# Six positions instead of five in the last column transform: the second MLP layer of two hidden units moved there

## The chip, the cores and the metric

One core of one Trainium2 chip runs the kernel. The metric is the time of one execution on the device in microseconds, here the median of three runs. TensorE (PE) multiplies matrices, VectorE (DVE) and ScalarE (ACT) do elementwise work and move results out of the accumulators, GpSimd (POOL) and SyncE (SP) mostly issue DMA transfers.

## The reference

A layer norm feeds two branches, which are added to the input: the real part of a two-dimensional Fourier transform, and an MLP with a gelu. S = 2048 rows, D = 640 columns, F = 1536 hidden units.

```python
x = A_x                                     # (1, 2048, 640)
xn = _layernorm(x, axis=-1)
a = xn @ dft_hid_re ; b = xn @ dft_hid_im
y = dft_seq_re @ a - dft_seq_im @ b
h = gelu(xn @ B_w1 + B_b1)
return x + y + (h @ B_w2 + B_b2)
```

## The kernel before

**Precision.** Each fp32 operand is split into a high part (a copy on ACT, `high`) and a low part (a subtraction on DVE, `low`, which reads the high part). A product (`product`, lines 298 to 303) is three matmuls into one accumulator: high x high, high x low of the moving operand, low x high of the weights. So the second matmul of a product needs the low part of the moving operand.

**Tiles.** The rows are cut into 4 row blocks of 512 (t = 0 to 3), the hidden units into 12 units of 128 (NF = 12), the columns into 5 chunks of 128 (ND = 5). A matmul has a 128x128 weight tile and a 128x512 moving tile. The second layer of one unit of one row block (`output`) is 5 chunks of one product each, 15 matmuls.

**Stages, in order.** (1) Row block 0 goes through the MLP plainly, unit by unit. (2) Row blocks 1 and 2 go through the first layer together: `pair(k)`, k = 0 to 5, makes units 2k and 2k+1 of both with sums and differences of operands, so that fewer matmuls do; seven `window` calls write three accumulator banks in turn. Of row block 1 the second layer is done inside the following pair (`put_out`); the hidden values of row block 2 are kept in DRAM (`gs`, by `keep`) and loaded again later (`load_unit`). Beside the pairs ACT and DVE prepare the forms of the column transform's matrix (`prep_w`, tiles named `wst`), which `beside_pair` calls at fixed places. (3) A loop over p = 0 to 13 does the rest of the second layer: p = 0 and 1 units 10 and 11 of row block 1, p = 2 to 13 units 0 to 11 of row block 2. Each iteration calls `output(g)` and then `split_unit(g + 2, units[p])`, which splits the unit that is wanted two iterations later. (4) Row block 3 goes through the MLP, while the forms of the sequence transform are built (`fourier_step`). (5) Sequence transform stages ("s") and column transform stages ("y") alternate, for pairs of row blocks; what the MLP left is added into the accumulators as seeds. The last "y" stage is that of row blocks 1 and 2.

**Beside the loop of (3).** `between(p)` makes the input of row block 3: statistics of the rows (`ln_stats` 12 to 15), the root on ACT (`ln_scale`, L224) and the normalization on DVE (`ln_apply`, L233) at p = 3, then 16 DMA transfers from SBUF to SBUF (`put_z`, L795, eight issued by SP and eight by POOL, tile `z`), 32x32 transposes on DVE (`transpose_z`, L261, `ztx`) and splits into `xt` (`prep_xt`) at p = 7, 8 and 9. It also stores seeds (partial sums, `keep_seed`), and reloads pieces of w1 (`load_w1`, `prep_w1`).

**The last column transform.** Seven products of sums are formed from the two row blocks' real and imaginary sequence sums (`form` makes and splits the moving operand of each). Each product has 5 positions along the contraction of 640 (two halves of 256 with two positions each, and an odd one of 128); its width in column chunks is (3, 3, 3, 2, 2, 2, 3), 18 in all (`GWIDE`). `hidden_entry` issues them; product 6's second chunk is done in two halves of 256 columns, so that the first half can leave early. `t2`, `t3`, `t4` form the sums on DVE.

What sets the order is the program text alone: each engine works through its instructions in the order in which the functions above issue them, and waits on semaphores. `place(name)` gives a region of SBUF a new use.

Of the kernel before, what the change touches and what calls it, by code (L numbers as in the profile page):

```python
# [22 lines left out]
PADL = 7  # L23


@with_exitstack
def kernel(
# [84 lines left out]
    seeds = dram.tile([P, 2 * ND, TB], F32, name="seeds")  # L112

# [193 lines left out]
    NG = NT * NF  # L307
    HT, oacc, xo = {}, {}, {}
# [56 lines left out]
    def output(g, es=range(ND)):  # L365
        t, i = divmod(g, NF)
        oacc[t] = [bank(k) for k in OBANKS[t]]
        hs = HT[g]
        for e in es:
            cols = slice(e * P, (e + 1) * P)  # L370
            product(
                oacc[t][e], (W2[i][:, 0, cols], W2[i][:, 1, cols]), (hs[:, 0], hs[:, 1]), i == 0, i == NF - 1
            )
# [589 lines left out]
    def keep(g, a):  # L963
        nc.gpsimd.dma_start(gs[g % NF], a)
# [42 lines left out]
    def beside_pair(k, at):  # L1007
# [54 lines left out]
        if k == LASTK and at == 7:  # L1062
            A["gs"] = place("xab3", (P, 5, TB), F32)
            for i in range(3, 6):
                load_unit(i)
        if k == LASTK and at == 2:
            for i in range(3):
                load_unit(i)
        if k == LASTK and at == 4:
            load_x(14)  # L1070
            load_x(15)
            for i in range(6, 8):
                load_unit(i)
            A["s1"] = place("xab2", (P, ND, TB), F32)
# [3 lines left out]
    def load_unit(i):  # L1078

        if i < NF:  # L1080
            units[i] = A["gs"][:, i - 3] if 3 <= i < 8 else early.tile([P, TB], F32, tag="w2r", bufs=3, name=f"g{i}")
            nc.sync.dma_start(units[i], gs[i])

    def pair(k):
# [13 lines left out]
        split_unit(a1, u, lambda _: high(zc, z_))  # L1098
# [25 lines left out]
        gelu(a2, x_)  # L1124
# [4 lines left out]
        for es in ((0, 1, 2), (3, 4)) if k == 0 else (range(ND),):  # L1129
            outputs.extend((g, e) for g in (a1, a2) for e in es)  # L1130

    def between(p):

        if p == 0:
            ln_stats(12)
            ln_stats(13)
        if p == 1:
            with_bias(A["s1"][:, 1], 1, 3)
            with_bias(A["s1"][:, 4], 1, 4)
            keep_seed("us", A["s1"][:, 4:])  # L1140
            ln_stats(14)
        if p == 2:
            ln_stats(15)
        if p == 3:
            ln_scale(NC)
            Z["z"] = zo_tile("z3")
            for c in range(3 * NC, 4 * NC):
                ln_apply(c)
            put_z(Z["z"], row_places, nc.gpsimd, nc.sync)
            new_xt(3)  # L1150
        if p == 4:
            with_bias(A["s1"][:, 0], 1, 2)
            keep_seed("x", A["s1"][:, :2])
        if p == 5:
            for e in range(2):
                less(A["s1"][:, 2 + e], 1, e, A["s1"][:, e])
            keep_seed("y", A["s1"][:, 2:4])
        for j in {7: (0,), 8: (1, 2), 9: (3, 4)}.get(p, ()):
            if j == 0:
                transpose_z("x30", Z["z"], 0)  # L1160
            if j + 1 < ND:
                transpose_z(f"x3{j + 1}", Z["z"], j + 1)
            prep_xt(f"x3{j}", j)
        if p == 11:
            open_place(*PLACES[3])
        if p == 12:
            open_place(*PLACES[2])
        for n in {0: (0,), 4: (1,), 5: (2,), 6: (3,), 7: (4,), 8: (5,), 9: (6,), 10: (7,), 11: (8,), 12: (9, 10), 13: (11,)}.get(p, ()):
            prep_w1(AGAIN[n], 2 * NF + n)
            load_w1(2 * NF + 3 + n)  # L1170
        if p in (0, 1, 4, 8):
            load_unit({0: 8, 1: 9, 4: 10, 8: 11}[p])
        if p == 10:
            put_rows(3, row_places, nc.sync)
        if p == 12:
# [61 lines left out]
    for p in range(2 + NF):  # L1237
        g = 2 * NF - 2 + p
        if p == NF:
            output(g)  # L1240
            gelu(g + 2, hidden(g + 2))
        elif p == NF + 1:
            acc = hidden(g + 2)
# [8 lines left out]
            gelu(g + 2, acc, fill)  # L1252
# [8 lines left out]
        else:  # L1261
            output(g, (3, 4, 0, 1, 2) if p == 1 else range(ND))
# [9 lines left out]
    for i in range(NF):  # L1272
        g = 3 * NF + i
        if i >= NF - 2:
            output(g)
        else:
            acc = hidden(g + 2)
            gelu(g + 2, acc)
            output(g)

        fourier_step(i)
# [109 lines left out]
    def seed(dst, src):  # L1391
        nc.scalar.activation(dst, src, AF.Copy)

    def beside(h, t, n):
# [108 lines left out]
        else:  # L1503
# [35 lines left out]
            if p == 3:  # L1539

                def load_d():
# [7 lines left out]
                    11: [lambda: seed(z_, A["seed"]), lambda: load_seeds("us", "vs")],  # L1549
# [42 lines left out]
    def hidden_beside(b, n):  # L1592
# [10 lines left out]

        def t2(k):
            return lambda: add(s(1, KU[k]), s(1, KV[k]), s(1, KU[k]), ALU.subtract)

        def t3(k):
            return lambda: add(s(0, KU[k]), s(1, KU[k]), s(0, KU[k]), ALU.subtract)

        def t4(k):  # L1610
            return lambda: add(s(0, KV[k]), s(0, KV[k]), s(1, KU[k]), ALU.subtract)
# [51 lines left out]
        def last_columns():  # L1663

            A["end"] = A["rt2"][:, 0, 0, 0]
# [56 lines left out]
        }.get(n, [])  # L1722
        sooner = 2 if last else 0
# [38 lines left out]
    def hidden_entry(n, b, w, u):  # L1762
        last = b == len(blocks) - 1
        where = (X, Y, Z, X, Z, X, X)[w]

        def use_g(acc, j, pos, first, stop, goes_on=False, rows=slice(None)):
            k = pos % 2
            a = form_slot(n - u + pos // 2)
            use(acc, GT[b, w * ND + pos], j, a, k, first, stop, goes_on, rows)

        def wide(j, pos):
            use_g(bank(where + j), j, pos, w < 3 and pos == 0 and not last, pos == ND - 1, w > 2 or last)

        mine = (2 * u, 2 * u + 1) if u < 2 else (4,)
        if w == 6 and last:

            if u == 0:
                for pos in range(ND):
                    use_g(bank(VS), 2, pos, False, pos == ND - 1, True)
                for pos in range(ND):  # L1780
                    wide(0, pos)
            elif u == 1:
                for acc, rows in zip((Y, X + 1), PARTS):
                    for pos in range(ND):
                        use_g(bank(acc)[:, rows], 1, pos, False, pos == ND - 1, True, rows)
# [7 lines left out]
        for pos in mine:  # L1793
            if w < 2:
                use_g(bank(US), 2, pos, w == 0 and pos == 0 and not last, w == 1 and pos == ND - 1, last)
# [4 lines left out]
        for pos in mine:  # L1800
# [80 lines left out]
```

## Time and profile before

| | |
|---|---|
| median of 3 runs | 850.13 us (849.91 to 850.81) |
| the profiled execution | 850.44 us |
| its span | 848.6 us |
| PE | 841.7 us busy, 3725 matmuls |
| DVE | 676.9 us, 889 instructions |
| ACT | 368.2 us, 527 instructions |
| POOL | 78.2 us, 142 instructions |

The span runs from the first to the last instruction of the profiled execution; its own time is 1.84 us longer. Row times are microseconds from the start of the span. In the timeline a row gives the start, the duration, the engine, the line, the operation and the tiles, with `x3` where like instructions follow each other. In the rows by group the two numbers behind the bar are the busy time in us and the mean of one instruction in ns. In the rows by stretch each engine has its busy time and its count, in the order PE, weight loads, DVE, ACT, POOL, then the granted clock of PE, the share of the DMA engines and GB/s. Matmul durations overlap: how fast PE goes is read from the starts.

### The profile page before, as it was taken

What the parts mean: (1) busy time and instruction counts of PE and PEld (TensorE: products, weight loads), DVE (VectorE), ACT (ScalarE), POOL (GpSimd) and SP (SyncE); (2) the same over time, 40 slices, a digit from 0 to 9 for tenths busy, and PEclk for the clock granted to TensorE, in tenths of its full rate; (3) what the DMA queues carried; (4) which work ended last, traced back from release to release, by engine and by line L of the source; (5) the groups of instructions that cost most, each with busy time, mean ns of one, the idle gap of its engine ahead of it and who ended that gap; (6) DMA issues with size and microseconds to landing.
All of it is one profiled execution on the core that took longest, in us unless ns stands there. A gap on an engine that the chain in (4) does not pass through costs nothing.

```text
span 848.6 us, 10664 instructions
## 1 busy us (share of the span) xinstructions
PE 841.7 (99%) x3725; PEld 696.9 (82%) x3725; DVE 676.9 (80%) x889; ACT 368.2 (43%) x527; POOL 78.2 (9%) x142
## 2 busy tenths in 40 slices
PE   9999999999999999999999999999999999999997
PEld 7888888888888888888888888888888888888886
DVE  6969989766643778979988887889967998886596
ACT  7546657545453555443444344232323433234340
POOL 3340024222200000000000000000000000000012
PEclk9999999999999999999999999999999999999999
DMA  7995767878785897958644679663845799916473
GB/s 232 280 251 153 151 178 246 261 223 305 198 220 139 344 313 143 204 129 190 152 137 110 165 226 285 158 147 96 224 142 156 229 246 245 310 43 229 149 192 88
DMA packets 193878, 167.33 MB, mean 197 GB/s; under 512 B 57792, under 2 KB 164800, under 8 KB 193312
## 3 DMA queue, kind: packets, MB, share of 16 engines
q1 hardware_dynamic: 182816, 136.89, 60.8%
q0 software_dynamic: 8832, 29.24, 10.1%
q10 hardware_dynamic: 2176, 0.52, 0.3%
q8 instruction: 29, 0.48, 0.2%
q14 instruction: 25, 0.20, 0.1%
HBM read 116.53 MB, written 46.14 MB: 192 GB/s over the span
## 4 chain that ended last, share of the span: by engine, by line
PE 99%; POOL 0%; DVE 0%; issue 0%; POOLq 0%
PE banks L302 30%; PE banks L303 30%; PE banks L304 29%; PE banks L322 10%; PE banks L685 1%; PE banks L701 0%; POOL warm L673 0%; POOL zeros L671 0%; DVE yo L1842 0%; PE banks L755 0%; POOLq masks.py:199 0%; POOLq L1867 0%
## 5 line engine op out<-in xcount | busy, mean ns | idle before, releaser
L188 ACT ACTIVATE as<-r 128x1024 fp32r<-128x1024 f32 x80 | 85.0, 1062 | 170.2 <-PE banks L304 146.4
L303 PE MATMUL banks<-as,xab 128*128 128x512 f32 (+1 forms) x389 | 150.5, 387 | 0.0
L304 PE MATMUL banks<-as,xab 128*128 128x512 f32 (+1 forms) x389 | 150.5, 387 | 0.0
L302 PE MATMUL banks<-as,xab 128*128 128x512 f32 (+1 forms) x389 | 150.5, 387 | 0.0
L191 DVE TENSOR_TENSOR as<-r,as 128x1024 fp32r<-128x1024 f32 x80 | 97.2, 1216 | 38.0 <-ACT as L188 37.8
L302 PE MATMUL banks<-as,xc 128*128 128x512 f32 x224 | 87.1, 389 | 0.0
L303 PE MATMUL banks<-as,xc 128*128 128x512 f32 x224 | 87.1, 389 | 0.0
L304 PE MATMUL banks<-as,xc 128*128 128x512 f32 x224 | 87.1, 389 | 0.0
L303 PEld LDWEIGHTS banks<-as,xab 128*128 128x128 f32 x389 | 73.0, 188 | 15.0
L302 PEld LDWEIGHTS banks<-as,xab 128*128 128x128 f32 x389 | 73.0, 188 | 14.8
L304 PEld LDWEIGHTS banks<-as,xab 128*128 128x128 f32 x389 | 73.0, 188 | 14.8
L188 ACT ACTIVATE as<-rt 128x1024 fp32r<-128x1024 f32 x32 | 34.0, 1062 | 72.5 <-PE banks L304 57.9
L322 PE MATMUL banks<-xt,xab 128*128 128x512 f32 x240 | 56.6, 389 | 0.0
L191 DVE TENSOR_TENSOR hs<-ab,hs 128x512 fp32r<-128x512 f32 x36 | 24.8, 689 | 38.0 <-ACT hs L188 37.5
L322 PEld LDWEIGHTS banks<-xt,xab 128*128 128x128 f32 x240 | 45.0, 188 | 9.3
L303 PEld LDWEIGHTS banks<-as,xc 128*128 128x128 f32 x224 | 42.0, 188 | 8.8
L304 PEld LDWEIGHTS banks<-as,xc 128*128 128x128 f32 x224 | 42.0, 188 | 8.7
L302 PEld LDWEIGHTS banks<-as,xc 128*128 128x128 f32 x224 | 42.0, 188 | 8.7
L302 PE MATMUL banks<-hs,xc 128*128 128x512 f32 x120 | 46.7, 389 | 0.0
L303 PE MATMUL banks<-hs,xc 128*128 128x512 f32 x120 | 46.7, 389 | 0.0
L304 PE MATMUL banks<-hs,xc 128*128 128x512 f32 x120 | 46.7, 389 | 0.0
L191 DVE TENSOR_TENSOR as<-rt,as 128x1024 fp32r<-128x1024 f32 x32 | 38.8, 1213 | 6.5 <-ACT as L188 6.5
(286 smaller groups left out, 1682.0 us busy)
## 6 DMA issues: line engine op xcount, KB each, us to landing
raw<-in_A_dft_seq_re_dram SPq DMA_DIRECT2D x64, 256.0 KB, 5.6
raw<-in_A_dft_seq_im_dram SPq DMA_DIRECT2D x64, 256.0 KB, 5.2
w1r<-in_B_w_dram SPq DMA_DIRECT2D x144, 80.0 KB, 3.1
wit<-wst POOLq DMA_DIRECT2D x15, 384.0 KB, 4.0
wit<-wst POOLq DMA_DIRECT2D x20, 256.0 KB, 4.2
forms_ab<-xab SPq DMA_DIRECT2D x4, 1280.0 KB, 7.7
xab<-wit SPq DMA_DIRECT2D x13, 384.0 KB, 4.8
row<-xn SPq DMA_DIRECT2D x14, 320.0 KB, 5.2
```

The source lines that it names most:

```text
L188: nc.scalar.activation(h, s, AF.Copy)
L191: nc.vector.tensor_tensor(l, s, h.bitcast(F32), op=ALU.subtract)
L302: nc.tensor.matmul(acc, wh, mh, start=first, stop=False, skip_group_check=goes_on)
L303: nc.tensor.matmul(acc, wh, ml, start=False, stop=False, skip_group_check=goes_on)
L304: nc.tensor.matmul(acc, wl, mh, start=False, stop=last, skip_group_check=goes_on)
L322: nc.tensor.matmul(acc, W1[i][:, a, j * P : (j + 1) * P], XT[j][:, b], start=n == 0, stop=n == len(steps) - 1)
L685: nc.tensor.matmul(wacc, warm[:, :P], warm, start=True, stop=True)
```

## The change

Units 10 and 11 (the last two, `NU = NF - 2 * NX` = 10 remain) of row blocks 1 and 2 no longer go through `output`. Their hidden values are written to DRAM (`late_units`) and loaded by POOL, with the two 128-row blocks of w2 that belong to them, at step 11 of the last sequence stage (`load_late`). In the last column transform they are a sixth position: they take the part that a real and an imaginary chunk take elsewhere, so `form` splits one more 128x512 tile for each of the seven products, `also` does the sums of `t2` to `t4` on the hidden values too, and `late_form` makes and splits the seven forms of w2.

The loop of stage (3) becomes p = 2 to 11. The splits of row block 2's units 0 and 1 move into the last pair, statistics to p = 2 and 3, the transposes of z to p = 6, 7 and 8, and the list of w1 pieces is shifted.

The core of the diff:

```diff
+NX = 1
+    late_units = dram.tile([P, 2, 2, NX, TB], F32, name="late_units")
+    NU = NF - 2 * NX
+    COUNT = (NF, NU, NU, NF)
...
                 split(a[:, 0, 0], a[:, 1, 0], src)
+                if n >= LASTY:
+                    split(a[:, 0, 1], a[:, 1, 1], A["h"][which, names is KV])
...
     def keep(g, a):
-        nc.gpsimd.dma_start(gs[g % NF], a)
+        t, i = divmod(g, NF)
+        if i < NU:
+            nc.gpsimd.dma_start(gs[i], a)
+        else:
+            nc.gpsimd.dma_start(late_units[:, t - 1, i % 2, (i - NU) // 2], a)
...
         if k == LASTK and at == 7:
             A["gs"] = place("xab3", (P, 5, TB), F32)
             for i in range(3, 6):
                 load_unit(i)
+            A["s1"] = place("xab2", (P, ND, TB), F32)
+            split_unit(2 * NF, units[0])
...
             for i in range(6, 8):
                 load_unit(i)
-            A["s1"] = place("xab2", (P, ND, TB), F32)
+            split_unit(2 * NF + 1, units[1])
...
         window(x_, b, 0, "t4", False, (b, 2, "oa0"))
-        gelu(a2, x_)
+        if k == LASTK:
+            with_bias(A["s1"][:, 1], 1, 3)
+            with_bias(A["s1"][:, 4], 1, 4)
+            keep_seed("us", A["s1"][:, 4:])
+        if 2 * k < NU:
+            gelu(a2, x_)
+        else:
+            keep(a2, unit(a2, x_))
...
-        if p == 0:
+        if p == 2:
             ln_stats(12)
             ln_stats(13)
-        if p == 1:
-            with_bias(A["s1"][:, 1], 1, 3)
-            with_bias(A["s1"][:, 4], 1, 4)
-            keep_seed("us", A["s1"][:, 4:])
+        if p == 3:
             ln_stats(14)
-        if p == 2:
             ln_stats(15)
-        if p == 3:
             ln_scale(NC)
...
-        for j in {7: (0,), 8: (1, 2), 9: (3, 4)}.get(p, ()):
+        for j in {6: (0,), 7: (1, 2), 8: (3, 4)}.get(p, ()):
...
-    for p in range(2 + NF):
+    for p in range(2, 2 + NU):
         g = 2 * NF - 2 + p
...
-            output(g, (3, 4, 0, 1, 2) if p == 1 else range(ND))
+            output(g, (0, 1, 3, 4, 2) if p == 2 else range(ND))
             split_unit(g + 2, units[p])
         between(p)
...
+    def load_late():
+
+        t = place("rt2", (P, 4096), F32)
+        A["end"] = t[:, :TB]
+        h = t[:, TB : 5 * TB].rearrange("p (t v k n) -> p t v k n", t=2, v=2, k=NX)
+        A["h"] = {(a, bool(v)): h[:, a, v, 0] for a in range(2) for v in range(2)}
+        nc.gpsimd.dma_start(h, late_units)
+        lo = 5 * TB
+        for v in range(2):
+            A["w2", v] = t[:, lo + v * D : lo + (v + 1) * D]
+            nc.gpsimd.dma_start(A["w2", v], w2[(NU + v) * P : (NU + v + 1) * P, :])
+        A["w2sum"] = t[:, lo + 2 * D : lo + 2 * D + 2 * P]
...
+    def late_form(w):
...
+        g = GH[w] = A["gh"][:, lo : lo + 2 * n * P].rearrange("p (a b) -> p a b", a=2)
+        if w == 2:
+            add(both, i2, r2)
+            add(r4, r4, i4)
+            add(r2, r1, r2, ALU.subtract)
+            add(r1, both, r1, ALU.subtract)
+            add(i1, i1, r1, ALU.subtract)
+        main, odd = {0: (r1, r4), 1: (i1, i4), 2: (both, r4), 3: (r1, None), 4: (i1, None), 5: (r2, None), 6: (i2, i4)}[w]
+        split(seen(g[:, 0, : 2 * P]), seen(g[:, 1, : 2 * P]), main)
...
+        def also(k, f, *of):
+
+            f(*(s(b, (KU, KV)[v][k]) for b, v in of))
+            if last and k == 2:
+                f(*(A["h"][b, bool(v)] for b, v in of))
...
+        if last:
+            forms_at = {0: (0,), 1: (1,), 3: (2,), 5: (3,), 7: (4,), 12: (5,), 14: (6,)}
+            post += [lambda w=w: late_form(w) for w in forms_at.get(n, ())]
...
+        NPOS = ND + NX if last else ND
...
-            use(acc, GT[b, w * ND + pos], j, a, k, first, stop, goes_on, rows)
+            use(acc, GT[b, w * ND + pos] if pos < ND else GH[w], j, a, k, first, stop, goes_on, rows)
...
-        mine = (2 * u, 2 * u + 1) if u < 2 else (4,)
+        mine = (2 * u, 2 * u + 1) if u < 2 else range(4, NPOS)
```

**Where the order changes.** PE at the end of the last pair, before. The `w1f` rows are the last window's, `hs_1878` is unit 10 of row block 1, `rt_782` holds w2:

```order
671 L304 MATMUL banks<-xab_605,w1f 128x512
672 L302 MATMUL banks<-hs_1878,rt_782 128x512
673 L303 MATMUL banks<-hs_1878,rt_782 128x512
674 L304 MATMUL banks<-hs_1878,rt_782 128x512
675 L302 MATMUL banks<-hs_1878,rt_782 128x512
```

The same place on PE in the changed kernel, where `hs_1975` is unit 0 of row block 2:

```order
671 L306 MATMUL banks<-xab_606,w1f 128x512
672 L304 MATMUL banks<-hs_1975,xc_177 128x512
673 L305 MATMUL banks<-hs_1975,xc_177 128x512
674 L306 MATMUL banks<-hs_1975,xc_177 128x512
675 L304 MATMUL banks<-hs_1975,xc_177 128x512
```

Thirty matmuls of row block 1 (the five rows above are the first of them) have gone from between the last window and unit 0 of row block 2.

ACT around the end of the last pair, before. `wst` are the pieces of the column transform's matrix, `hs_2024` the high part of unit 0 of row block 2 (`g_1862`), `ab_1996` the gelu of row block 1's unit 11:

```order
216 L188 ACTIVATE wst_4_1964<-row 128x256
217 L188 ACTIVATE wst<-row 128x256
218 L342 ACTIVATE ab_1996<-banks,b1c 128x512
219 L188 ACTIVATE hs_1998<-ab_1996 128x512
220 L188 ACTIVATE hs_2024<-g_1862 128x512
221 L188 ACTIVATE xab_2006<-w1r_1606 128x640
```

The same place on ACT in the changed kernel, where `hs_1975`, `hs_2009` and `hs_2030` are the high parts of units 0, 1 and 2:

```order
215 L190 ACTIVATE wst_4_1963<-row 128x256
216 L190 ACTIVATE wst<-row 128x256
217 L190 ACTIVATE hs_1975<-g_1863 128x512
218 L1002 ACTIVATE xab_1974<-banks,b2c 128x512 x2
219 L346 ACTIVATE ab_2002<-banks,b1c 128x512
220 L190 ACTIVATE hs_2009<-g_1865 128x512
221 L190 ACTIVATE hs_2030<-g_1867 128x512
```

Unit 0's copy now follows the last `wst` copy directly; the bias copies (L992 before, L1002 now) stand ahead of the gelu.

DVE around the transposes of z, before. `hs_2232` is the low part of unit 7 of row block 2, `hs_2263` that of unit 8:

```order
309 L191 TENSOR_TENSOR hs_2207<-xab_1971,hs_2207 128x512
310 L191 TENSOR_TENSOR xab_2007<-w1r_2035,xab_2007 128x640
311 L191 TENSOR_TENSOR hs_2232<-xab_1971,hs_2232 128x512
312 L261 STREAM_TRANSPOSE ztx_2235<-z_2113 128x512
313 L261 STREAM_TRANSPOSE ztx_2237<-z_2113 128x512
314 L191 TENSOR_TENSOR xt_2134<-ztx_2235,xt_2134 128x512
315 L191 TENSOR_TENSOR as<-w1r_2157,as 128x640
316 L191 TENSOR_TENSOR hs_2263<-g_2040,hs_2263 128x512
```

The same place on DVE in the changed kernel, where `hs_2172` is unit 6 and `hs_2203` unit 7:

```order
306 L193 TENSOR_TENSOR xab_2013<-w1r_1785,xab_2013 128x640
307 L193 TENSOR_TENSOR hs_2172<-xab_1970,hs_2172 128x512
308 L263 STREAM_TRANSPOSE ztx_2175<-z_2078 128x512
309 L263 STREAM_TRANSPOSE ztx_2177<-z_2078 128x512
310 L193 TENSOR_TENSOR xt_2099<-ztx_2175,xt_2099 128x512
311 L193 TENSOR_TENSOR xab_2013<-w1r_2041,xab_2013 128x640
312 L193 TENSOR_TENSOR hs_2203<-xab_1970,hs_2203 128x512
```

The transposes, which wait for all z transfers, now stand ahead of unit 7's low part, where they stood ahead of unit 8's.

More of the change, by code (lines that the diff above doesn't have):

```diff
@@ L1097, in pair @@
         zc = mr.tile([P, TB], F32, tag="zt", bufs=2, name=f"zc{k}") if k else early.tile([P, TB], F32, tag="w2r", bufs=3, name="zc0")
-        split_unit(a1, u, lambda _: high(zc, z_))
+        if 2 * k < NU:
+            split_unit(a1, u, lambda _: high(zc, z_))
+        else:
+            keep(a1, u)
+            high(zc, z_)
         if k:
@@ L1279 @@
             output(g)
+        if i == 0:
+            between(2 + NU)
         fourier_step(i)
@@ L1392, in seed, with seen @@
         nc.scalar.activation(dst, src, AF.Copy)
+    def load_late():
[9 more added lines that the diff above has]
+        A["w2sum"] = t[:, lo + 2 * D : lo + 2 * D + 2 * P]
+    GH = {}
+    def late_form(w):
+        def seen(ap):
+            return ap.rearrange("p (c q i) -> p c q i", q=Q, i=B)
+        if w == 0:
+            A["gh"] = place("xc23", (P, 13 * 2 * P))
+        r, i = (A["w2", v].rearrange("p (q c i) -> p c q i", q=Q, i=B) for v in range(2))
+        (r1, r2, r4), (i1, i2, i4) = ((m[:, 0:2], m[:, 2:4], m[:, 4:5]) for m in (r, i))
+        both = seen(A["w2sum"])
+        n = GWIDE[w]
+        lo = {0: 0, 1: 3, 2: 6, 3: 9, 4: 11, 5: 0, 6: 3}[w] * 2 * P
+        g = GH[w] = A["gh"][:, lo : lo + 2 * n * P].rearrange("p (a b) -> p a b", a=2)
[7 more added lines that the diff above has]
+        split(seen(g[:, 0, : 2 * P]), seen(g[:, 1, : 2 * P]), main)
+        if odd is None:
+            return
+        h, l = (seen(g[:, k, 2 * P :]) for k in range(2))
+        if w < 6:
+            split(h, l, odd)
+        else:
+            nc.scalar.activation(h, odd, AF.Copy, scale=-1.0)
+            nc.vector.scalar_tensor_tensor(l, odd, -1.0, h.bitcast(F32), op0=ALU.mult, op1=ALU.subtract)
     def beside(h, t, n):
@@ L1768, in use_g @@
             a = form_slot(n - u + pos // 2)
-            use(acc, GT[b, w * ND + pos], j, a, k, first, stop, goes_on, rows)
+            use(acc, GT[b, w * ND + pos] if pos < ND else GH[w], j, a, k, first, stop, goes_on, rows)
         def wide(j, pos):
-            use_g(bank(where + j), j, pos, w < 3 and pos == 0 and not last, pos == ND - 1, w > 2 or last)
-        mine = (2 * u, 2 * u + 1) if u < 2 else (4,)
+            use_g(bank(where + j), j, pos, w < 3 and pos == 0 and not last, pos == NPOS - 1, w > 2 or last)
+        mine = (2 * u, 2 * u + 1) if u < 2 else range(4, NPOS)
         if w == 6 and last:
             if u == 0:
-                for pos in range(ND):
-                    use_g(bank(VS), 2, pos, False, pos == ND - 1, True)
-                for pos in range(ND):
+                for pos in range(NPOS):
+                    use_g(bank(VS), 2, pos, False, pos == NPOS - 1, True)
+                for pos in range(NPOS):
                     wide(0, pos)
@@ L1783, in hidden_entry @@
                 for acc, rows in zip((Y, X + 1), PARTS):
-                    for pos in range(ND):
-                        use_g(bank(acc)[:, rows], 1, pos, False, pos == ND - 1, True, rows)
+                    for pos in range(NPOS):
+                        use_g(bank(acc)[:, rows], 1, pos, False, pos == NPOS - 1, True, rows)
             return
@@ L1794, in hidden_entry @@
             if w < 2:
-                use_g(bank(US), 2, pos, w == 0 and pos == 0 and not last, w == 1 and pos == ND - 1, last)
+                use_g(bank(US), 2, pos, w == 0 and pos == 0 and not last, w == 1 and pos == NPOS - 1, last)
             if w == 2:
```

48 lines of the change are left out of this document (26 added, 22 removed).

## The prediction

> **What bounds the kernel now.** I read the page first: busy times, the slices, the chain that ended last.
>
> ```profile
> span 848.6 us, 10664 instructions
> PE 841.7 (99%) x3725; PEld 696.9 (82%) x3725; DVE 676.9 (80%) x889; ACT 368.2 (43%) x527; POOL 78.2 (9%) x142
> PEclk9999999999999999999999999999999999999999
> PE 99%; POOL 0%; DVE 0%; issue 0%; POOLq 0%
> ```
>
> PE works through the span at full clock and is nearly the whole chain that ended last. Next the waits of PE, of which there is one, and two pieces of the chain: the 18 warm-up matmuls and 15 matmuls of a unit.
>
> ```profile
> PE banks L685 <- POOL warm L673: 2.0, 1, 2.0
> ...
> 1.98 6.38 PE banks L685 x18
> 24.46 3.40 PE banks L322 x15
> ```
>
> So PE never waits after 2 us, every helper engine just keeps ahead, and two things move the time: how many PE steps there are, and whether the new order makes PE wait. A 128x512 step is 3.40/15 = 0.2267 us, and a unit's second layer (5 chunks x 3 matmuls) is 3.40 us. The narrow matmuls are in PE's timeline of the tail:
>
> ```profile
> 840.02 0.28 PE L302 MATMUL banks<-as,xab 128*128 128x256 f32 x1
> ...
> 841.45 0.28 PE L302 MATMUL banks<-r,xab 128*128 128x256 f32 x1
> ```
>
> From the one to the other there are 12 steps: 1.43/12 = 0.12 us for a 128x256 step.
>
> **The change part by part.** The profiled execution took 850.44 us, of which 848.6 are the span and 1.84 lie around it; the median of the three timed runs is 850.13. All sums below are in the span, and the difference is put on the median.
>
> *The matmuls (A).* Units 10 and 11 of two row blocks lose their second layer: 4 units x 15 = 60 steps, 60 x 0.2267 = 13.60 us. The sixth position costs 18 column products x 3 = 54, of which one product is done in two halves: 51 wide and 6 narrow steps, 51 x 0.2267 + 6 x 0.12 = 12.28 us. A = -1.32 us. That is 0.155% of the time; 0.2%, or 1.7 us, is about what a measurement of this kernel can tell from no change. So even with no new wait nothing could be called faster, and waits decide.
>
> *The wait for unit 0 (B).* Here is PE at the end of the last pair, then ACT and DVE beside it.
>
> ```profile
> 199.91 0.39 PE L304 MATMUL banks<-xab,w1f 128*128 128x512 f32 x1
> 200.14 0.39 PE L302 MATMUL banks<-hs,rt 128*128 128x512 f32 x1
> ...
> 206.94 0.39 PE L302 MATMUL banks<-hs,xc 128*128 128x512 f32 x1
> ```
> ```profile
> 200.28 1.19 ACT L188 ACTIVATE wst<-row 128x256 fp32r<-128x256 f32 x3 [1.29 <-DVE row L465]
> 201.37 0.67 ACT L342 ACTIVATE ab<-banks,b1c 128x512 f32<-128x512 f32 x1
> 202.07 0.63 ACT L188 ACTIVATE hs<-ab 128x512 fp32r<-128x512 f32 x1
> ...
> 204.42 1.37 ACT L992 ACTIVATE xab<-banks,b2c 128x512 f32<-128x512 f32 x2
> ```
> ```profile
> 200.73 1.22 DVE L191 TENSOR_TENSOR wst<-row,wst 128x256 fp32r<-128x256 f32 x3
> 202.74 0.69 DVE L191 TENSOR_TENSOR hs<-ab,hs 128x512 fp32r<-128x512 f32 x1 [0.79 <-ACT hs L188]
> ```
>
> After the last window (L304, 199.91) PE has 30 matmuls on block 1's units 10 and 11 (hs,rt), to 206.94. They are just the removed ones, and they cover ACT and DVE, which are still splitting the last W-transform pieces (wst). With them gone, the matmul due at 200.14 is unit 0 of block 2. Its high half stands in ACT's order behind those three wst copies, so it starts at 201.37, where the gelu started, takes 0.63 and is there at 202.00: 1.9 late. Its low half needs the high one (202.74 follows 202.07 + 0.63 by 0.04), so it runs 202.04 to 202.73; PE needs it for the second matmul, due at 200.37. With some 0.05 to PE, B = 202.78 - 200.37 = 2.4 us. The wst chain itself hangs on earlier windows of PE and does not move. Bounds: 1.8 (the high half alone, a little sooner) and 2.6. Behind it on ACT come two bias copies and the last gelu, which free the banks of unit 0's third to fifth chunk: 202.0 + 1.37 (the row at 204.42) + 0.67 = 204.1, sooner than PE reaches them. On PE the whole rest of the program stands behind this wait.
>
> *The wait for unit 7 (C).* Block 3's normalized rows go through DMAs (z) and come back as transposes on DVE. In this order the splits of unit 7 stand behind them on DVE and ACT; before, those of unit 8 did. The steps before: the last row statistics, the square root, the z transfers, the transposes, the split.
>
> ```profile
> 210.26 0.89 DVE L217 BATCH_NORM_STATS2 st<-row 128x6 f32<-128x320 f32 x2
> ...
> 211.18 0.21 DVE L218 BATCH_NORM_AGGREGATE mv<-st 128x2 f32<-128x12 f32 x1
> ...
> 213.65 2.18 DVE L233 TENSOR_SCALAR row<-row,mv 128x640 f32<-128x640 f32 x4
> ...
> 228.21 1.30 DVE L261 STREAM_TRANSPOSE ztx<-z 128x512 f32<-128x512 f32 x2 [2.71 <-DMA w1r<-in_B_w_dram]
> ...
> 230.99 0.68 DVE L191 TENSOR_TENSOR hs<-g,hs 128x512 fp32r<-128x512 f32 x1
> ...
> 234.84 0.69 DVE L191 TENSOR_TENSOR hs<-g,hs 128x512 fp32r<-128x512 f32 x1
> ```
> ```profile
> 211.19 1.28 ACT L224 ACT_TABLE_LOAD   x1
> 212.49 0.30 ACT L224 ACTIVATE mv<-mv,eps 128x4 f32<-128x4 f32 x1
> ...
> 230.12 0.61 ACT L188 ACTIVATE hs<-g 128x512 fp32r<-128x512 f32 x1
> ```
> ```profile
> L795 SPq DMA_DIRECT2D z<-row x8: 594/722/1800, 215.9 to 221.2; - x8
> L795 POOL DMA_DIRECT2D z<-row x8: 550/551/575, 216.1 to 220.0; - x8
> ...
> DMA to landing us min/median/max: 2.1/3.5/6.6
> ```
> ```profile
> 234.14 0.39 PE L302 MATMUL banks<-hs,r 128*128 128x512 f32 x1
> ```
>
> The last z lands at 221.2 + 6.6 = 227.8, and the transposes start 0.4 later. (DVE's 2.71 us of idle time is put down to a w1r load; its instruction waits for all sixteen z transfers, and they landed last.) The low half of the unit behind them ends 231.67 - 228.21 = 3.46 us after they start, at 231.67, and PE wanted it at 234.14 + 0.23: 2.7 us of slack.
>
> In the new order the transposes come one unit earlier and PE comes two units (6.8 us) earlier. PE wants unit 7's low half at 200.14 + 7 x 3.40 + 2.4 + 0.23 = 226.57. What starts the chain hardly moves: the rows of block 3 are loaded as early as before, and their statistics end at 211.4 as before. One thing is gained: the table load (211.19) stood behind a split that waited for PE, so the root came 1.1 after the statistics. In the new order it stands behind unit 3's split, which needs only the end of unit 0 on PE (205.9); the root comes at 211.4, and all that follows is 1.1 earlier: transposes at 227.1, low half at 230.57, with 0.05 to PE at 230.62. C = 230.62 - 226.57 = 4.05 us. Bounds: if the last z took the median 3.5 instead of 6.6, 3.1 us less, so 0.95; if the root comes no sooner, 5.1. I take the middle one because the z transfers, their queues and the seeds written behind them are as before. In ACT's queue the splits for the next units and block 3's pieces stand behind, which delays nobody but PE.
>
> *One unit on (D).* The next unit's low half starts 234.84 - 230.99 = 3.85 us after this one, since two more transposes and their splits lie between; PE takes 3.40. D = +0.45 while PE is tied to that chain. After that there is one transpose less, and PE is no longer held.
>
> *The last column transform.* The sixth position needs its own splits: 27 DVE instructions and 18 ACT copies more. Rows of that stage, and a split:
>
> ```profile
> 800.00:844.00 44.00, 43.77 (x208) 36.67 (x206) 36.45 (x42) 11.94 (x13) 7.76 (x12) 1.00 0.54 144
> L191 DVE TENSOR_TENSOR hs<-ab,hs 128x512 fp32r<-128x512 f32 x36 | 24.8, 689 | 38.0 <-ACT hs L188 37.5
> L465 DVE TENSOR_TENSOR banks<-banks,rt 128x256 f32<-128x256 f32 x2 | 0.9, 427 | 0.0
> ```
>
> In the row by stage DVE (third) is busy 36.45 us of 44. Added are 11 instructions of 128x512 at 0.69 (seven low halves, four sums), 12 of 128x256 at 0.43 or less, 4 of 128x128, which I take at under 0.43: at most 7.6 + 16 x 0.43 = 14.5 us. PE's stretch grows by 12.3. DVE then works 51 of 56.3 us, ACT far less. Every form is made a product or more ahead of its use, and hidden values and w2 blocks are loaded a stage ahead, by POOL, behind which only seeds stand that are wanted later. I cost this stage at nothing; if that cover is gone see the third rival. The other loads of units and of w1 pieces move with the loop by a place or two and keep their distance; the tail is untouched.
>
> Sum: -1.32 + 2.4 + 4.05 + 0.45 = +5.6 us. On the median: 850.13 + 5.6 = **855.7 us** (on the profiled execution's own time 856.0).
>
> **The rivals.**
>
> 1. *The z transfers land sooner.* For it: the shortest z took 2.1 us, and the one to 6.6 was issued when seeds were being written too. With the median 3.5 for the last: -1.32 + 2.4 + 0.95 + 0.45 = +2.5, 852.6 us. With 2.1, C and D vanish: +1.1, 851.2 us, which is no measurable change. Against it: neither queue is changed. [...]
>
> 2. *Not slower: both waits are covered.* If ACT got to unit 0's copy before the last wst copies (by 1.9 us), and the chain of z were 4.1 us shorter, only A is left: 848.8 us, within 0.2%. It decides where the halves are there at 200.14 and 226.3. Against it: the order of instructions on ACT puts wst first, and 4.1 us is more than the root gains.
>
> 3. *DVE becomes the bound of the last stage.* If none of DVE's 7.55 us of idle time in that row can be used, 44 + 14.5 = 58.5 against 56.3 on PE: +2.2 more, 857.9 us. Against it: its idle time there is mostly waiting for PE's banks.
>
> 4. *The long wait C lets the clock fall.* At the start of the kernel 18 warm-ups took 6.38 us instead of 18 x 0.2267 = 4.08: 2.3 us lost until the clock was full. C is one idle stretch of some 3.4 us before the high half. If the clock fell there: +2.3 more, 858.0 us. Against it: no wait in the trace of before has that length, so it shows neither. [...]
>
> 5. *The change doesn't save matmuls.* The order of instructions has 3724 matmul rows instead of 3727, with six narrow ones; this can hardly fail.
>
> **How the numbers follow.** Chances: the forecast 0.53; rival 1 with the median 0.14, with 2.1 us 0.06; rival 2 0.07; rival 3 0.08; rival 4 0.08; a gain of over 1.7 us that I don't see in the profile 0.04; rival 5 next to nothing. Left out of the range are 848.8, 851.2 and that gain (0.17); it reaches from a little below 852.6 to rival 4, 851.6 to 858.0, which holds the bounds of B and C too (-0.6 to +0.2 and -3.1 to +1.05). Faster by over 0.2%: 0.04. Within 0.2%: rival 2 and the second case of rival 1, 0.13. Slower: the rest, 0.83.
>
> **What would show it.** In the profile of the changed kernel: PE waits for ACT hs and DVE hs just after the last w1f matmul, together about 2.4 us; a second wait for hs some 24 us later, about 4 us, behind DVE's ztx transposes; a third of about 0.4 one unit later; none in the last 60 us; PE busy some 840.4 us. I am wrong if z lands under 10 us after its first issue, if hs of unit 0 stands ahead of wst in time, if PEclk drops after the second wait, or if PE waits in the last stage.

## The result, and the profile after

The changed kernel took 857.32 us (median of 6 runs, 856.42 to 858.04), the kernel before 850.21 (849.91 to 850.81): a ratio of 1.0083, interval 1.007 to 1.0096, or 7.1 us more. The forecast was 855.7, with 851.6 to 858.0 as its range. The profiled execution took 856.42, its span 854.6.

The page's busy times, the waits of PE in the changed kernel, and the rows by stretch from 245 us on (PE's busy time and count come first in each):

```profile
span 854.6 us, 10699 instructions
PE 842.9 (99%) x3722; PEld 697.0 (82%) x3722; DVE 685.9 (80%) x912; ACT 372.0 (44%) x541; POOL 80.7 (9%) x147
```
```profile
PE banks L304 <- ACT hs L190: 4.7, 2, 2.9
PE banks L691 <- POOL warm L679: 2.0, 1, 2.0
PE banks L305 <- DVE hs L193: 0.7, 2, 0.4
PE banks L707 <- ACT xp L740: 0.3, 1, 0.3
```
```profile
245.00:780.00 535.00, 535.00 (x2362) 443.01 (x2361) 442.15 (x463) 208.01 (x249) 6.50 (x12) 1.00 0.72 196
780.00:848.00 68.00, 68.00 (x309) 56.62 (x308) 55.44 (x76) 24.33 (x37) 8.28 (x13) 1.00 0.45 126
```

Before, the only wait was the 2.0 us at the start. Now there are two waits for a high part (4.7 us, the longest 2.9) and two for a low part. The 0.3 us for `xp` lies in the first 10 us of the kernel and is no part of the argument: the last window ends no later than before (below). From 245 us on PE is busy in every microsecond, 535.00 of 535 and 68.00 of 68, at a granted clock of 1.00: the sixth position runs without a stall. All that was lost was lost before 245.

PE, ACT and DVE of the changed kernel at the end of the pairs:

```profile
199.84 0.39 PE L306 MATMUL banks<-xab,w1f 128*128 128x512 f32 x1
201.95 0.49 PE L304 MATMUL banks<-hs,xc 128*128 128x512 f32 x1 [1.73 <-ACT hs L190]
202.68 0.50 PE L305 MATMUL banks<-hs,xc 128*128 128x512 f32 x1 [0.23 <-DVE hs L193]
203.02 0.39 PE L306 MATMUL banks<-hs,xc 128*128 128x512 f32 x1
```
```profile
200.25 1.13 ACT L190 ACTIVATE wst<-row 128x256 fp32r<-128x256 f32 x3 [1.34 <-issue]
201.29 0.61 ACT L190 ACTIVATE hs<-g 128x512 fp32r<-128x512 f32 x1
```
```profile
201.93 0.69 DVE L193 TENSOR_TENSOR hs<-g,hs 128x512 fp32r<-128x512 f32 x1
```

The third matmul of unit 0 on PE was due at 199.84 + 3 x 0.2267 = 200.52 and started at 203.02: the first wait costs 2.50 us. The copy stands right behind the three `wst` copies, as the order of instructions has it.

The same engines some 25 us later, around the transposes of z:

```profile
226.91 1.30 DVE L263 STREAM_TRANSPOSE ztx<-z 128x512 f32<-128x512 f32 x2 [7.97 <-DMA g<-gs]
...
229.69 0.69 DVE L193 TENSOR_TENSOR hs<-xab,hs 128x512 fp32r<-128x512 f32 x1
...
233.54 0.69 DVE L193 TENSOR_TENSOR hs<-g,hs 128x512 fp32r<-128x512 f32 x1
```
```profile
226.16 0.39 PE L306 MATMUL banks<-hs,r 128*128 128x512 f32 x1
229.49 0.49 PE L304 MATMUL banks<-hs,r 128*128 128x512 f32 x1 [2.93 <-ACT hs L190]
230.43 0.50 PE L305 MATMUL banks<-hs,r 128*128 128x512 f32 x1 [0.45 <-DVE hs L193]
230.77 0.39 PE L306 MATMUL banks<-hs,r 128*128 128x512 f32 x1
...
231.46 0.47 PE L306 MATMUL banks<-hs,r 128*128 128x512 f32 x1
...
232.16 0.63 PE L305 MATMUL banks<-hs,r 128*128 128x512 f32 x1
232.59 0.63 PE L306 MATMUL banks<-hs,r 128*128 128x512 f32 x1
...
235.11 0.40 PE L306 MATMUL banks<-hs,r 128*128 128x512 f32 x1
235.34 0.40 PE L304 MATMUL banks<-hs,r 128*128 128x512 f32 x1
235.57 0.39 PE L305 MATMUL banks<-hs,r 128*128 128x512 f32 x1
```

DVE's 7.97 us of idle time is put down to a load of a unit, but that load had landed only at 226.95, just after the transposes began. They wait for all sixteen z transfers, of which the last was issued at 219.62, took 6.8 us and landed at 226.40, 0.5 us ahead of them. On PE the third matmul of unit 7 was due at 226.16 + 3 x 0.2267 = 226.84 and started at 230.77: the second wait costs 3.93 us. Then the steps are 0.43 us long (232.16 to 232.59) where they had been 0.23. The granted clock (the number behind POOL's) in the stretches around it:

```profile
224.00:231.00 7.00, 3.62 (x16) 2.45 (x14) 3.99 (x7) 2.30 (x4) 0.00 (x0) 1.00 0.60 179
231.00:235.00 4.00, 4.00 (x12) 3.16 (x11) 3.97 (x7) 2.42 (x5) 0.00 (x0) 0.58 0.35 91
235.00:245.00 10.00, 10.00 (x45) 8.25 (x45) 5.21 (x8) 6.15 (x9) 1.09 (x2) 1.00 0.73 213
```

The clock fell at about 231.6, some 2 us after PE had come back to work (229.49), and was full again at 235.0. From 231.46 to 235.11 there are 9 steps, which took 3.65 us instead of 9 x 0.2267 = 2.04: 1.61 us lost.

The sum, by the last matmul, before and now:

```profile
843.49 0.28 PE L304 MATMUL banks<-r,xab 128*128 128x256 f32 x1
```
```profile
850.18 0.28 PE L306 MATMUL banks<-r,xc 128*128 128x256 f32 x1
```

Matmuls -1.32, first wait +2.50, second +3.93, clock +1.61, a last window that came 0.07 sooner (199.84 for 199.91): 6.65, and 850.18 - 843.49 = 6.69. Behind the last matmul the span went on for 854.6 - 850.2 = 4.4 us, before for 5.1; what makes this 0.7 no run shows. The profiled execution is the fastest of the six, and the median is another 0.9 up. Its mean granted clock is 0.997; in the other five it is 0.995 (four of them) or 0.996. Over some 855 us, 0.002 less is, by estimate, 3.4 us more at half clock, or 1.7 us of time. So most of the six seem to have had a second fall of the clock, or one twice as long; no profile of this kernel shows either.

### The profile page after: what moved, and what is told of

It is laid out like the page before. It is cut to its first block, busy times and chain, and to the rows that moved or that the text cites. A ratio compares the mean times of both kernels' runs of the same rounds, so it can differ in the third digit from the quotient of the medians.

```text
span 854.6 us, 10699 instructions
## 1 busy us (share of the span) xinstructions
PE 842.9 (99%) x3722; PEld 697.0 (82%) x3722; DVE 685.9 (80%) x912; ACT 372.0 (44%) x541; POOL 80.7 (9%) x147
## 4 chain that ended last, share of the span: by engine, by line
PE 92%; issue 2%; DVE 2%; DMA 1%; ACT 1%; SPq 1%; POOL 1%; POOLq 0%; ACTq 0%
PE banks L305 27%; PE banks L306 27%; PE banks L304 27%; PE banks L326 10%; DMA g<-gs 1%; SPq L801 1%; DMA row<-in_A_x_dram 0%; POOL wit L444 0%; DVE st L219 0%; DVE hs L193 0%; DMA wit<-wst 0%; PE banks L707 0%; DVE row L469 0%; DVE row L235 0%; DVE xab L193 0%
## 5 line engine op out<-in xcount | busy, mean ns | idle before, releaser
L304 PE MATMUL banks<-as,xc 128*128 128x512 f32 x234 | 91.0, 389 | 0.0
L305 PE MATMUL banks<-as,xc 128*128 128x512 f32 x234 | 91.0, 389 | 0.0
L306 PE MATMUL banks<-as,xc 128*128 128x512 f32 x234 | 91.0, 389 | 0.0
L190 ACT ACTIVATE as<-rt 128x1024 fp32r<-128x1024 f32 (+1 forms) x36 | 36.5, 1015 | 78.1 <-PE banks L306 59.3
L304 PEld LDWEIGHTS banks<-as,xc 128*128 128x128 f32 x234 | 43.9, 188 | 9.1
L305 PEld LDWEIGHTS banks<-as,xc 128*128 128x128 f32 x234 | 43.9, 188 | 9.1
L306 PEld LDWEIGHTS banks<-as,xc 128*128 128x128 f32 x234 | 43.9, 188 | 9.1
L193 DVE TENSOR_TENSOR as<-rt,as 128x1024 fp32r<-128x1024 f32 (+1 forms) x36 | 41.5, 1153 | 9.0 <-ACT as L190 9.0
```

What stands on the lines that cost most here:

```text
L190: nc.scalar.activation(h, s, AF.Copy)
L193: nc.vector.tensor_tensor(l, s, h.bitcast(F32), op=ALU.subtract)
L304: nc.tensor.matmul(acc, wh, mh, start=first, stop=False, skip_group_check=goes_on)
L305: nc.tensor.matmul(acc, wh, ml, start=False, stop=False, skip_group_check=goes_on)
L306: nc.tensor.matmul(acc, wl, mh, start=False, stop=last, skip_group_check=goes_on)
```

## The experiments

The theory: the first wait comes from ACT's and DVE's order at the end of the pairs, the second from the chain of rows, root, z, transposes and split, which doesn't depend on PE; and the fall of the clock follows from the second wait. The rivals: the waits are independent and add up; the z transfers are slow by their own queue; the fall has nothing to do with the wait. Times are medians, beside some 850.4 for the kernel before on the same chips; the diffs show the core of each edit, with the rest marked by dots.

**The transposes one iteration later.**

```diff
-        for j in {6: (0,), 7: (1, 2), 8: (3, 4)}.get(p, ()):
+        for j in {7: (0,), 8: (1, 2), 9: (3, 4)}.get(p, ()):
```

> The changed kernel with the transposes of z one iteration later (7, 8, 9 for 6, 7, 8), so that unit 8 and not unit 7 is split behind them. Theory (the second wait comes from the place of the transposes in DVE's and ACT's order): PE reaches unit 8 just 3.4 us later, so the wait falls from 3.9 to about 0.4, one more of about 0.4 follows, the clock stays at 1.00 (1.6 us), and block 3's first layer finds its input in time or waits up to 0.5; the time falls by 4.5 to 5, to about 852.5. Rival (PE then waits for block 3's input as long as it did for unit 7): 856 to 857.

852.56 us (851.93 to 853.35; ratio 1.0026, 1.0017 to 1.0035). PE's waits for hs:

```profile
202.23 0.50 PE L304 MATMUL banks<-hs,xc 128*128 128x512 f32 x1 [1.73 <-ACT hs L190]
202.96 0.50 PE L305 MATMUL banks<-hs,xc 128*128 128x512 f32 x1 [0.22 <-DVE hs L193]
```

Only the first is left; the second and the two smaller ones that I had expected are gone, and PE did not wait for block 3's input. One number in a table was worth 4.8 us. But the clock, expected to stay at 1.00, fell to half at about 203.85 for 3.4 us in this execution, behind the first wait: PE's steps, 0.23 us until then, were 0.43 from 204.10 to 207.08 and 0.23 again from 207.40 on. It made PE come some 1.6 us later to unit 8, so this trace can't show whether the two smaller waits arise where the clock stays up. The three runs with the lowest mean granted clock (0.997; 852.2 to 852.8) are no slower than the others, which would fit: what the clock costs ahead of the transposes is then not waited for behind them.

**The seeds behind z.**

```diff
-            keep_seed("x", A["s1"][:, :2])
+            keep_seed("x", A["s1"][:, :2], nc.sync)
...
-            keep_seed("y", A["s1"][:, 2:4])
+            keep_seed("y", A["s1"][:, 2:4], nc.sync)
```

> The changed kernel with the two seed transfers of 512 KB issued by SP behind its z transfers, not by POOL beside them. Theory (SP's last z transfers are late because the seeds share the DMA engines with them): the last z lands some 2.5 us sooner after the first issue (12.0 to about 9.5), the second wait falls from 3.9 to about 1.4, too short for the clock to fall, 1.6 us more; together about 4 us less, 853. Rival (SP's own queue is the limit): the last z lands 12 us after the first issue as before, no change, 857.

852.65 us (852.29 to 853.33; 1.0028, 1.0016 to 1.0039). The time to landing of the z transfers in the changed kernel, then in this one, and this one's transposes:

```profile
DMA to landing us min/median/max: 2.1/3.5/6.8
```
```profile
DMA to landing us min/median/max: 2.1/3.4/4.6
```
```profile
223.39 1.30 DVE L263 STREAM_TRANSPOSE ztx<-z 128x512 f32<-128x512 f32 x2 [4.48 <-DMA z<-row]
```

With two transfers of 512 KB out of the way the slowest z took 4.6 us for 6.8, and the transposes, whose idle time the trace now puts down to z, started 3.5 us sooner (223.39 for 226.91). In the changed kernel the late ones were SP's last two z, issued at 218.84 and 219.62: they took 5.2 and 6.8 us, in flight together with the seeds (issued at 219.24 and 219.79, landed at 224.33 and 226.16). What was left of the second wait were idle times of 0.17 and 0.15. So 3.5 us of the wait of the transposes came from transfers beside z that nobody was waiting for yet; I had expected 2.5. By what mechanism the seeds delay z no run shows.

**Work for PE in the second wait.**

```diff
+            if p == 9:
+                for _ in range(14):
+                    nc.tensor.matmul(bank(0), W2[0][:, 0, :P], HT[g - 1][:, 0], start=True, stop=True)
             output(g, (0, 1, 3, 4, 2) if p == 2 else range(ND))
```

> The changed kernel with 14 matmuls more (into an accumulator bank that is free) ahead of unit 7's output, 3.2 us of PE work in its wait of 3.9. Theory (the granted clock of 0.5 from 231.6 to 235.0 follows from PE idling for 2.9 us in one piece): with PE at work the clock stays 1.00, unit 8 comes up to 1.7 us sooner and then waits some 0.35 for its low half; the time falls by about 1.3 us though 14 matmuls are added, 856. Rival (the fall of the clock has nothing to do with that wait): the clock falls again and the time is the same or up to 0.2 longer.

855.67 us (855.26 to 855.93): 1.65 less than the changed kernel, with 14 matmuls more. Its stretch behind the wait:

```profile
231.00:235.00 4.00, 3.79 (x16) 2.84 (x16) 3.96 (x8) 2.30 (x4) 0.00 (x0) 1.00 0.29 82
```

The clock is 1.00 where it had been 0.58, and the mean granted clock of all five runs is 0.998 or more. So the fall in the changed kernel came with PE's idle time there. The second wait itself stayed, since PE still waited 0.26 and 0.44 for unit 7's halves behind the added work.

**The first wait alone, three ways.** First the last step of the W preparation behind the splits of units 0 and 1:

```diff
-            steps = {3: (0,), 7: (1, 2)}
+            steps = {3: (0,), 7: (1,), 4: (2,)}
...
+        if k == LASTK and at == 4:
+            split_unit(2 * NF + 1, units[1])
         for n in steps.get(at, ()):
...
```

> The changed kernel with the last step of the W preparation in the last pair issued after unit 0's and unit 1's splits. Theory (the second wait is tied to the z transfers, not to PE, so what PE gains at the first wait it loses at the second): the wait for hs of unit 0 falls from 2.5 us to about 1.0, the one behind the transposes grows by as much (3.9 to about 5.4), and the time stays within 0.4 us of the changed kernel, 857. Rival (the waits add up independently): the second wait stays 3.9 and the time falls by 1.5 us.

858.22 us (857.42 to 859.04), no better than the changed kernel (856.42 to 858.04) and by the medians 0.9 worse. The first wait fell to 0.83, but the transposes started at 228.47 for 226.91. The last two row loads of block 3 go into memory that the W preparation works in: SP waited 3.0 us for DVE's `wst` before it could issue them, 0.5 in the changed kernel, and issued them 2.6 us later. I had moved a step without asking what else waits for its memory. A wait of 1.53 at unit 4 came on top; the second wait was 3.9 in one piece, with 6.8 us at half clock around it.

Then 12 matmuls of row block 1 behind the last window:

```diff
-        put_out(10)
+        put_out(0 if k == LASTK else 10)
         window(x_, b, 0, "t4", False, (b, 2, "oa0"))
+        put_out(10)
...
```

> The changed kernel with the last 12 matmuls of row block 1's second layer issued behind the last window of the pairs, so that they lie where the 30 removed ones lay; nothing else. Theory (the first wait is the lack of cover, and the second is tied to z): the wait for hs of unit 0 is gone, the second one grows by 2.5 us to 6.4, with an idle stretch of more than 5 us, and the time is not better than the changed kernel's: 857 to 859. Rival (the waits add up): 854.8.

856.81 us (856.42 to 858.93): no better, but not for the reason given. The first wait was not gone:

```profile
201.92 0.51 PE L304 MATMUL banks<-hs,xc 128*128 128x512 f32 x1 [0.65 <-ACT hs L190]
```

Unit 0 started at 201.92 as in the changed kernel (201.95). PE has the same work to do ahead of it in either order, so moving 12 matmuls only moved part of the idle time ahead of the last window, which now waited 0.8 for a bank. The second wait did not grow either (2.90 for 2.93), since PE came to it no sooner. Cover is work that PE has over and above, and the change had taken that away.

Third, units 0 and 1 split ahead of the W preparation, their first two chunks multiplied first, and the loads of units 4 and 5 behind those of the rows:

```diff
+        if k == LASTK and at == 7:
+            split_unit(2 * NF, units[0])
+            split_unit(2 * NF + 1, units[1])
         for n in steps.get(at, ()):
...
+            if p == 2:
+                output(g, (0, 1))
+                output(g + 1, (0, 1))
+            output(g, (3, 4, 2) if p < 4 else range(ND))
...
```

> The changed kernel with only the first three of those edits (units 0 and 1 split ahead, their first chunks first, the loads of units 4 and 5 behind the rows). Theory (the second wait is tied to z, not to PE): the first wait falls to about 0.5 and the second grows from 3.9 to about 5.9, so the time stays at 857, or more where the clock falls for longer. Rival (the waits add up): 855.3.

857.78 us (856.45 to 857.96). Its waits:

```profile
203.52 0.50 PE L304 MATMUL banks<-hs,xc 128*128 128x512 f32 x1 [0.48 <-ACT xab L1002]
215.27 0.50 PE L305 MATMUL banks<-hs,xc 128*128 128x512 f32 x1 [0.34 <-DVE hs L193]
230.15 0.79 PE L304 MATMUL banks<-hs,r 128*128 128x512 f32 x1 [4.59 <-ACT hs L190]
```

The first wait is cut to 0.48, the second grew to 4.59 in one piece, and the clock stayed at half for 6.8 us instead of 3.4. What PE gains at a wait it gives back at the next one that does not hang on PE. The waits do not add up; if they did, the time would have been 855.3.

**Both edits for the second wait** (the two short diffs above together).

> The changed kernel with the seeds behind z on SP and the transposes one iteration later, both at once. Theory (all of the second wait and of the clock's fall after it comes from the z chain): no wait for hs behind the transposes is left, only the first wait of 2.5 us and the gain of 1.3 on the matmuls: 850.3 + 1.2 = 851.5, up to 853 if the clock falls behind the first wait in some executions. Rival (each of the two edits hits another limit, PE waits for block 3's input instead): no better than either alone, 852.6.

852.67 us (851.82 to 853.58), no better than either alone, as the rival had it, though not by its mechanism: no wait for block 3's input shows. The only wait for `hs` is the first. The profiled execution of this kernel took 853.42, and behind the first wait it shows

```profile
200.00:203.00 3.00, 1.05 (x5) 0.31 (x3) 2.71 (x6) 2.49 (x6) 2.42 (x5) 1.00 0.79 264
203.00:204.00 1.00, 1.00 (x4) 0.81 (x5) 0.00 (x0) 1.00 (x3) 0.70 (x2) 0.79 0.79 256
204.00:207.00 3.00, 3.00 (x9) 2.33 (x8) 2.52 (x6) 1.55 (x3) 0.69 (x2) 0.50 0.95 318
```

a clock of one half for some 3.4 us, about 1.6 us lost, as in the execution with the transposes alone. In the profile of the changed kernel the same first wait had left the clock alone (1.00 from 204 to 224). Only two of this kernel's ten runs (853.4 and 853.6, at 0.996 and 0.997) have a mean granted clock under 0.998, so by my estimate it fell here in some executions only.

**Work for PE in the first wait**, on top of those two:

```diff
+            if p == 2:
+                for _ in range(8):
+                    nc.tensor.matmul(bank(5), W2[0][:, 0, :P], HT[2 * NF - 3][:, 0], start=True, stop=True)
```

> The kernel of e6 (seeds behind z, transposes one iteration later) with 8 matmuls more, into a free accumulator bank, in PE's wait for unit 0, 1.8 us of its 2.5. Theory (in some executions the clock falls to half for 3.4 us behind the first wait of 1.7 us, which spreads e6's runs over 851.8 to 853.6): with PE at work it stays 1.00, the median falls by 0.8 to 1.2 us to about 851.6 and the runs lie within 1 us. Rival (the spread has another source, the transfers): the same median and spread as e6.

851.74 us; 9 of 11 runs lie between 851.46 and 852.11, two at 853.1 and 853.6. In the profile the clock stays at 1.00 behind the first wait, and no run is under 0.998. The median fell by 0.9, as the theory has it, but the clock alone doesn't give that: without their two runs at the lowest clock the ten above have a median of 852.4, 0.25 lower. So the fall behind the first wait fits the two slowest of those runs; where the rest of the 0.9 comes from is open, and so are the two slow runs here, whose clock is 0.999 and 1.000. Part of the difference between the two profiles, 0.46 of 1.82 us, arises in the first 10 us, where PE waited 0.8 for `xp` in the one and not in the other.

**The kernel before without its cover.** Here the second layer of units 10 and 11 of row block 1 is left out, so that part of the output is missing (the sums of that block end at unit 9).

```diff
-            output(g, (3, 4, 0, 1, 2) if p == 1 else range(ND))
+            if p > 1:
+                output(g)
...
```

> The kernel before with the second layer of units 10 and 11 of row block 1 left out (30 matmuls, 6.8 us; that part of the output is missing), nothing else changed. Theory (these matmuls cover ACT and DVE at that place): a wait of 2.4 us for unit 0, one of 1.7 for unit 8 behind the transposes and 0.45 for the next, so only 2.2 of the 6.8 us are gained: 848.1, more by 1.7 where the clock falls. Rival (PE bound, no cover needed): 6.8 less, 843.5.

849.16 us, 1.3 less than the kernel before (ratio 0.9988, 0.9979 to 0.9997), though 6.8 us of matmuls were gone.

```profile
203.40 0.79 PE L302 MATMUL banks<-hs,xc 128*128 128x512 f32 x1 [2.96 <-ACT hs L188]
```
```profile
203.00:207.00 4.00, 3.59 (x8) 2.50 (x9) 3.93 (x10) 3.16 (x6) 0.75 (x2) 0.50 0.86 285
207.00:210.00 3.00, 3.00 (x10) 2.36 (x9) 1.55 (x5) 0.00 (x0) 0.00 (x0) 0.60 1.04 411
```

The last window's last matmul started at 200.05, so the first of unit 0 was due at 200.28; it came at 203.40, 3.1 us late. The clock was at one half for some 6.8 us from 202.6 on, and 13 steps took 6.06 us instead of 2.95, another 3.1. Together that is nearly all of the 6.4 us that the profiled execution gave back (850.04; the median is 0.9 lower). PE came to the transposes so late that the second wait, which I had expected here too, never arose. So these matmuls were mostly free: they filled time that PE would have waited.

**All of it together.** Two attempts at a version that beats both: the edits of the third try at the first wait with those for the second, and then the seeds later still (both at p = 6 instead of 4 and 5; the expectation below calls that three iterations), with unit 4 split ahead of the row normalization.

> The changed kernel with units 0 and 1 of row block 2 split ahead of the last two steps of the W preparation, their first two chunks multiplied ahead of the rest, the loads of units 4 and 5 behind those of the last rows, the seeds behind z on SP and the transposes one iteration later. Theory (the first wait is ACT's and DVE's order, the second the z chain): the first wait falls from 2.5 us to about 0.5 (a bank that ACT frees after the W copies), the second is gone, the clock stays 1.00: 850.4 - 1.3 + 0.5 = 849.6. Rival (the W preparation is later by two splits, and so are the last rows and z): a second wait of 1 us or more is left, 851.

> The kernel of e10 with the two seed transfers three iterations later in SP's order, behind the w1 pieces, and unit 4 split ahead of the row normalization. Theory (what was left of the second wait in e10 came from the w1 pieces, which stood behind the seeds on SP and ahead of unit 8's split on ACT and DVE): no wait behind the transposes, none of 0.34 at unit 4, only the bank wait of 0.5 is left; 850.4 - 1.3 + 0.7 = 849.8. Rival (the w1 pieces are late by the z transfers themselves): 851.5 to 852 as in e10.

851.96 us (851.46 to 852.52; ratio 1.0018) and 851.81 (850.68 to 854.3; 1.0016, 1.0007 to 1.0025). In the first the clock stayed up, but a second wait was left, because the w1 piece that DVE and ACT split ahead of unit 8 now came late. In the second that piece was in time, but unit 4's early split waited for its load until 211.65, and the row normalization and z stood behind it: first z at 216.97 for 214.11, waits of 0.98 and 0.45. A third edit, 12 matmuls behind the last window and both edits for the second wait:

> The three edits together: the 12 matmuls behind the last window, the seeds behind z on SP, the transposes one iteration later. Theory (with both waits covered the matmuls saved are all that is left): no PE wait for hs over 0.2 us, clock 1.00 throughout, 850.3 - 1.3 = 849.0. Rival (the last column transform or block 3's input hides a further loss): 850.3 or more.

852.13 us (851.44 to 853.71), where I had expected 849.0. In its profile the waits are short (0.78 for a bank, 0.65 and 0.23 for unit 0, 0.41 for unit 4, 0.57 and 0.44 behind the transposes) and the clock stays up, but they are not gone. None of the three beats the kernel before. The matmuls bring 1.3 us, and each of these orders gave back 2.6 to 3.0.

## Why the prediction was right, and where it was off

- **The matmuls (A, -1.32).** Right by count, and the last matmul's start adds up with it to 0.04 us. The stage that pays for them has no wait, and DVE, at 55.44 of 68 us, did not bound it: rival 3 fell.
- **The wait for unit 0 (B, 2.4).** 2.50 measured, by the copy behind `wst` as worked out.
- **The wait for unit 7 (C, 4.05).** 3.93. The transposes were put at 227.1 and came at 226.91; the low half at 230.57 and came at 230.38. The root came at 211.01 for the 211.4 forecast. The z transfers were taken as before, and the last landed 12.0 us after the first issue; rival 1 (a shorter z) did not hold in this kernel, but the cause that it names (the seeds) was right, as the seeds' experiment shows.
- **One unit on (D, 0.45).** Did not arise: unit 8's low half ended at 234.23, and PE, at half clock, wanted it at 235.57. With the clock kept up by added matmuls PE did wait there, 0.16.
- **The clock (rival 4, given a chance of 0.08 and priced at +2.3).** This is the step that failed: the sum left the clock out. "No wait in the trace of before has that length, so it shows neither" was true, and I took it for a low chance. It fell, as one of the four signs of being wrong had it, and cost 1.61 behind the second wait. By the estimate from the mean granted clocks (0.995 or 0.996 for 0.997) most of the other runs had as much again. 850.2 - 1.3 + 2.5 + 3.9 + 1.6 = 856.9, and the longer time at half clock in most runs is enough for the 857.3. For one fall the price was too high: in the trace of before the warm-up steps took 0.43 us each for some 4.3 us (1.98 to 6.3, then 0.23), and here the clock was at half for some 3.4. PE's busy time came out at 842.9 for the 840.4 forecast, in part because slow steps count as busy (their rows last 0.63 us for 0.39). In the changed kernel's profile the clock fell after 2.93 us of idling and not after the first wait's 1.73; in the profiles of two experiments it fell after 1.73 and 1.72.

Range and sign held, and so did the mechanism of both waits. The closeness of the number is partly luck. For the profiled execution the forecast was 856.0 and 856.42 was measured, because D (0.45), which did not arise, and the shorter stretch behind the last matmul (0.7) made up most of the clock's 1.61. Against the median it is 1.6 low.

## What to carry to other kernels

Where PE is 99% of the chain that ended last, its matmuls are still not all worth their time: some are the cover under which other engines catch up, and taking those away gains little (1.3 us of 6.8 here). Before a step is moved or removed, work out for each consumer behind it when its operand is ready by what does not depend on PE, since a wait of that kind eats every gain made ahead of it. Look at the granted clock behind new idle time of PE before you price it: in the changed kernel it was at half for 3.4 us behind the wait of 2.93, which cost 1.61 us more. And look for transfers that nobody waits for yet beside those that somebody does: here two of them went with 6.8 us for the slowest z, which took 4.6 without.

## What the runs showed of the hardware

- In the changed kernel PE idled for 2.93 us and, after one matmul, for 0.45 more. Behind that the granted clock was 0.50 from 231.63 to 235.05, for 3.4 us; the fall came some 2 us after PE had gone back to work (back at 229.49, steps still 0.23 at 231.23, 0.43 from 231.73 on).
- Behind idle times of 2.96 us (the kernel before without its cover), 3.92 (the last W preparation step behind the splits) and 4.59 (units 0 and 1 split ahead) the clock was at half for some 6.8 us, each time from before PE was back: from about 202.6 for PE's 203.40, 230.9 for 231.05 and 229.6 for 230.15.
- Behind the first wait of 1.72 or 1.73 us the clock was at half for some 3.4 us in two profiles (the transposes one iteration later, and both edits for the second wait). In three others (the changed kernel, the seeds behind z, and the work for PE in the second wait) PE's steps there stayed at 0.23 us. What makes the difference no run shows.
- 14 matmuls into an unused bank, within the second wait, went with a clock of 1.00 from 231 to 235, where it had been 0.58, and the time fell by 1.65 us. With 8 in the first wait the clock stayed at 1.00 from 200 to 240 in the profile; of the 0.9 us by which the median fell, the two runs at the lowest clock account for 0.25.
- Sixteen SBUF to SBUF transfers of 80 KB, issued within 5.2 us on two queues, took from 2.1 us (the first) to 6.8 us (the last) in the changed kernel, where two 512 KB transfers were in flight beside the last of them. Without those two the slowest took 4.6.
